# Long-run loads with strided reads of the turned tiles, in a gated recurrence fused with a multiplicative feed-forward layer

## Chip, cores, metric

One core of a Trainium2 chip. The metric is the device time of one execution in microseconds (us).

## The reference, cut to what matters

```python
# x, r_gate, i_gate: (4, 5824, 256) float32; a_param: (256,)
log_a   = 8.0 * sigmoid(r_gate) * log(clip(sigmoid(a_param), 1e-6, 1 - 1e-6))
a_t     = exp(log_a)
x_gated = sqrt(max(1 - a_t * a_t, 1e-6)) * sigmoid(i_gate) * x
h = a_t[:, t] * h + x_gated[:, t]          # for each t in order; y[:, t] = h
out = (((y @ w1) * (y @ w2)) @ w3) @ w_out # y as 23296 tokens x 256
```

The recurrence runs along the tokens, so its two inputs, the decay `a` and the gated input, must lie in the order of time when it is scanned.

## The kernel before

23296 tokens pass in chunks of 512 (the first has 256). A chunk of r, i and x is loaded with tokens on partitions. Tanh makes the sigmoids, the tiles are turned so that features lie on partitions and tokens along the free dimension, and there decay, square, root, gated input and scan run. Two up-projections, their product and one down-projection (w3 and w_out are folded into one matrix at the start) give the output. The instruction order of every engine is computed ahead from estimated durations and is fixed.

```python
def load(c, nm):                       # nm is "r", "i" or "x"
    n = sizes[c] // P                  # P = 128
    t = loads.tile([P, 4, D], F32, name=nm + "_t", tag=nm)
    nc.sync.dma_start(
        out=t[:, :n, :],
        in_=src[nm][starts[c]:starts[c] + sizes[c], :].rearrange("(n p) c -> p n c", p=P))
    T[nm, c] = t
# ... tanh, plus-one and product with x; turned by PE into PSUM for c < NPE (6), else by a DMA transpose into SBUF
def decay(c, cb):                      # ACT, per half of the features
    nc.scalar.activation(out=T["a", c][:, cb, :w], in_=T["pr", c][:, cb, :w], func=AF.Exp,
                         scale=la4[:, cb:cb + 1], bias=la4[:, cb:cb + 1])
# ... square (GpSimd from chunk 4 on), root (ACT)
def gated(c):                          # VectorE; n and pu are both in SBUF from chunk 6 on
    nc.vector.scalar_tensor_tensor(
        out=T["n", c][:, :, :w], in0=T["n", c][:, :, :w], scalar=1e-3,
        in1=T["pu", c][:, :, :w], op0=ALU.max, op1=ALU.mult)
# ... scan (VectorE, two SBUF inputs), cast of h (GpSimd), up, copy (ACT), product (VectorE), down, evac, store
```

On VectorE's queue the gated inputs and scans of a later chunk stand between the products of the current one. A product that is late keeps a PSUM buffer, and PE waits for it (4.0 us in all before).

## Time and profile before

| | before |
|---|---|
| median of the first runs | 532.71 us (532.49 to 533.56) |
| profiled span | 530.9 us |
| PE, ACT, DVE, POOL busy | 94, 87, 84, 63% |
| chain that ended last | 81% PE |

PE, ACT, DVE and POOL are TensorE, ScalarE, VectorE and GpSimd; PEld is PE's loading of weights. In the views, pa and pb are the two up-projections in PSUM, sa is ACT's copy of pa, g_t is the product of sa and pb, po is the down-projection, a_t is the decay, nrm is the gated input, u_t is GpSimd's product of gate and x, h_t is the scan; rt and ut are turned tiles in SBUF, ptr is one in PSUM. Three views of before. First the windows of the steady stretch (columns: stretch, length, busy us and count of PE, PEld, DVE, ACT, POOL, then clock, DMA share, GB/s):

```profile
100.00:450.00 350.00, 348.05 (x2137) 208.89 (x2135) 309.06 (x241) 331.88 (x390) 262.02 (x200) 1.00 0.97 254
```

Then who waited for whom (us in all, times, longest us):

```profile
PE pa L227 <- DVE g_t L241: 4.0, 7, 1.7
...
PE pb L227 <- ACT sa L234: 1.1, 1, 1.1
```

And the decay's source line (ns minimum/median/maximum), with its source in SBUF (rt) and in PSUM (ptr):

```profile
L179 ACT ACTIVATE a_t<-rt,la x80: 798/815/851, 54.9 to 449.0; 128x512 f32<-128x512 bf16 x80
L179 ACT ACTIVATE a_t<-ptr,la x12: 556/770/787, 9.3 to 43.0; 128x512 f32<-128x512 bf16 x10, 128x256 f32<-128x256 bf16 x2
```

PE works through 348 of 350 us and hardly waits for the copies (sa, 1.1 us in all) and products (g_t, 4.0 us).

VectorE's gated inputs and scans, which read SBUF alone in the steady stretch, and GpSimd's instructions hold each other up. Before, a gated input of 1024 columns takes 1192 ns at least and up to 2340, a scan up to 2327, and GpSimd's square 1032 at least and up to 2048. The product g_t, whose second input is in PSUM, takes 1223 ns at most in all of its 184 records. The texts call the two engines, as far as they hold each other up, the port pair, and the time of such instructions port time.

### The profile page before, as it was taken

Reading aid. Unit: us, or ns where it says so; the run is one execution under the profiler, and the core shown is the slowest. Engines: PE = TensorE matmul, PEld = TensorE weight load, DVE = VectorE, ACT = ScalarE, POOL = GpSimd, SP = SyncE. Lnnn points to the kernel's source line nnn. Section 1 sums busy time; section 2 is a strip of 40 time slices with the busy share of each in tenths; the row PEclk is TensorE's granted clock in tenths of the full one; section 3 lists DMA queues with packets and bytes.
Section 4 is the critical chain, followed back from the end, with each engine's and each line's share of the span. In section 5 each row is a group of like instructions: output and inputs, shape, how many; then the busy total and the mean of one; then the engine's idle time right before and its main releaser. Section 6 shows DMA issues by size and latency. Waiting matters only on the chain.

```text
span 530.9 us, 8667 instructions
## 1 busy us (share of the span) xinstructions
PE 498.4 (94%) x3144; PEld 303.3 (57%) x3144; DVE 446.7 (84%) x367; ACT 463.1 (87%) x546; POOL 335.8 (63%) x260
## 2 busy tenths in 40 slices
PE   1568899999999999999999999999999999999997
PEld 1434565666565566565656565565665655566655
DVE  2998988997968899998999988789898889899641
ACT  6998879999999999999999899799998999965452
POOL 1338485887758686876859788578868578841000
PEclk9999999999999999999999999999999999999999
DMA  8998999999997996997997879999899787231112
GB/s 274 356 359 243 292 282 296 324 299 275 295 273 199 279 315 171 278 299 197 287 252 221 226 204 238 329 196 266 226 274 303 199 208 212 61 98 59 41 61 99
DMA packets 184939, 124.31 MB, mean 234 GB/s; under 512 B 88640, under 2 KB 182848, under 8 KB 184896
## 3 DMA queue, kind: packets, MB, share of 16 engines
q1 hardware_dynamic: 184624, 123.76, 86.4%
q8 instruction: 24, 0.39, 0.3%
q14 instruction: 19, 0.16, 0.1%
q10 hardware_dynamic: 272, 0.00, 0.0%
HBM read 78.91 MB, written 23.86 MB: 194 GB/s over the span
## 4 chain that ended last, share of the span: by engine, by line
PE 81%; DVE 8%; ACT 4%; issue 3%; DMA 3%; SPq 0%; DVEq 0%; ACTq 0%
PE pa L227 27%; PE pb L227 26%; PE po L248 26%; DVE g_t L241 2%; DMA rt<-th_r 2%; DVE h_t L211 2%; DVE w_t L276 1%; ACT sa L234 1%; PE pw L299 1%; ACT th_i L133 1%; DMA i_t<-in_i_gate_dram 1%; DVE nrm L196 1%; DVE u_t L148 1%; ACT ot L254 1%; ACT a_t L179 1%
## 5 line engine op out<-in xcount | busy, mean ns | idle before, releaser
L241 DVE TENSOR_TENSOR g_t<-sa,pb 128x1024 bf16<-128x1024 bf16 (+1 forms) x184 | 218.4, 1199 | 60.0 <-ACT sa L234 44.8
L227 PEld LDWEIGHTS <-w_sb 128*128 128x128 bf16 x1472 | 144.6, 98 | 149.1 <-issue 10.7
L234 ACT CAST sa<-pa 128x1024 bf16<-128x1024 f32 (+1 forms) x184 | 183.0, 999 | 32.8 <-PE pa L227 30.9
L227 PE MATMUL pa<-y_t,w_sb 128*128 128x512 bf16 (+1 forms) x736 | 188.7, 380 | 4.0 <-DVE g_t L241 4.0
L227 PE MATMUL pb<-y_t,w_sb 128*128 128x512 bf16 (+1 forms) x736 | 188.4, 379 | 2.9 <-DVE g_t L241 1.5
L248 PE MATMUL po<-wp_sb,g_t 128*128 128x256 bf16 x1456 | 181.7, 273 | 0.2 <-DVE nrm L196 0.2
L248 PEld LDWEIGHTS <-g_t 128*128 128x128 bf16 x1456 | 142.4, 98 | 46.0 <-issue 0.4
L211 DVE TENSOR_TENSOR_SCAN h_t<-a_t,h_t,nrm 128x512 f32<-128x512 f32 (+3 forms) x90 | 136.6, 1534 | 0.8
L187 POOL TENSOR_TENSOR nrm<-a_t 128x512 f32<-128x512 f32 x84 | 104.7, 1258 | 43.5 <-ACT a_t L179 43.2
L153 POOL TENSOR_TENSOR u_t<-th_i,x_t 128x512 bf16<-128x512 f32 x80 | 116.5, 1472 | 2.5
L219 POOL CAST y_t<-h_t 128x1024 bf16<-128x1024 f32 x38 | 44.6, 1173 | 67.9 <-DVE h_t L211 62.1
L138 POOL TENSOR_SCALAR th_i<-th_i 128x1024 f32<-128x1024 f32 x42 | 57.6, 1371 | 21.8 <-ACT th_i L133 21.8
L254 ACT COPY ot<-po 128x512 f32<-128x512 f32 x91 | 53.4, 587 | 16.3 <-PE po L248 15.6
L179 ACT ACTIVATE a_t<-rt,la 128x512 f32<-128x512 bf16 x80 | 63.5, 816 | 4.5 <-DMA rt<-th_r 4.2
L196 DVE SCALAR_TENSOR_TENSOR nrm<-nrm,ut 128x1024 f32<-128x1024 f32 x40 | 59.8, 1494 | 2.4 <-ACT nrm L191 2.4
L133 ACT ACTIVATE th_i<-i_t 128x1024 f32<-128x1024 f32 (+1 forms) x46 | 48.2, 1052 | 1.1 <-DMA i_t<-in_i_gate_dram 1.0
L191 ACT ACTIVATE nrm<-nrm 128x1024 f32<-128x1024 f32 (+1 forms) x46 | 48.1, 1056 | 0.8 <-DVE nrm L187 0.6
L126 ACT ACTIVATE th_r<-r_t 128x1024 bf16<-128x1024 f32 x40 | 42.3, 1063 | 2.1 <-DMA r_t<-in_r_gate_dram 2.0
L161 PE MATMUL ptr<-ident,th_r 128*128 128x128 bf16 x44 | 4.7, 269 | 16.7 <-DVE ident L73 8.7
L276 POOL CAST w_sb<-wf 128x1024 bf16<-128x1024 f32 x4 | 6.1, 1545 | 19.7 <-DMA wf<-in_moe_w_dram 19.7
L191 ACT ACT_TABLE_LOAD x14 | 18.0, 1283 | 0.2
L161 PEld LDWEIGHTS <-th_r 128*128 128x128 bf16 x44 | 3.7, 122 | 18.5 <-ACT th_r L124 14.9
(33 smaller groups left out, 127.1 us busy)
## 6 DMA issues: line engine op xcount, KB each, us to landing
out_dram<-ot SPq DMA_DIRECT2D x91, 256.0 KB, 3.6
r_t<-in_r_gate_dram SPq DMA_DIRECT2D x45, 512.0 KB, 5.3
i_t<-in_i_gate_dram SPq DMA_DIRECT2D x45, 512.0 KB, 5.2
x_t<-in_x_dram SPq DMA_DIRECT2D x45, 512.0 KB, 5.0
wf<-in_moe_w_dram SPq DMA_DIRECT2D x12, 512.0 KB, 5.7
wf<-in_moe_w_out_dram SPq DMA_DIRECT2D x2, 512.0 KB, 6.0
rt<-th_r SPq DMA_TRANSPOSE x40, 4.5
ut<-u_t SPq DMA_TRANSPOSE x40, 4.6
```

The lines of the kernel that those rows point to most:

```text
L138: nc.gpsimd.tensor_scalar(t, t, 1.0, 1.0, op0=ALU.add, op1=ALU.mult)
L153: nc.gpsimd.tensor_mul(out=u.rearrange("p cb j q -> p j cb q")[:, js], in0=cut(t)[:, js], in1=cut(T["x", c])[:, js])
L179: nc.scalar.activation(out=T["a", c][:, cb, :w], in_=T["pr", c][:, cb, :w], func=AF.Exp, scale=la4[:, cb:cb + 1], bias=la4[:, cb:cb + 1])
L187: eng.tensor_mul(out=T["n", c][:, cb, :w], in0=T["a", c][:, cb, :w], in1=T["a", c][:, cb, :w])
L191: nc.scalar.activation(out=T["n", c][:, :, :w], in_=T["n", c][:, :, :w], func=AF.Sqrt, scale=-1.0, bias=1.0)
L196: nc.vector.scalar_tensor_tensor(out=T["n", c][:, :, :w], in0=T["n", c][:, :, :w], scalar=1e-3, in1=T["pu", c][:, :, :w], op0=ALU.max, op1 ...
L211: nc.vector.tensor_tensor_scan(T["h", c][:, cb, lo:hi], T["a", c][:, cb, lo:hi], T["n", c][:, cb, lo:hi], init, ALU.mult, ALU.add)
L227: nc.tensor.matmul(out=pp[:, q, :w], lhsT=w_sb[:, cb, m * P:(m + 1) * P], rhs=T["y", c][:, cb, :w], start=(cb == 0), stop=(cb == NCB - 1))
L234: nc.scalar.copy(out=sa[:, :, :w], in_=T["pa", c, mp][:, :, :w])
L241: nc.vector.tensor_mul(out=T["g", c][:, 2 * mp:2 * mp + 2, :w], in0=T["sa", c, mp][:, :, :w], in1=T["pb", c, mp][:, :, :w])
L248: nc.tensor.matmul(out=T["po", c, j // 2][:, j % 2, :], lhsT=T["g", c][:, k, j * P:(j + 1) * P], rhs=wp_sb[:, k, :], start=(k == 0), stop= ...
L254: nc.scalar.copy(out=T["ot", c, j2], in_=T["po", c, j2])
```

## The change

The intent is longer DRAM runs. With `(n p)` a partition takes four tokens that lie 128 tokens apart, in runs of 1 KB; with `(p n)` it takes four neighbours in one run of 4 KB. After turning, column `j * 128 + q` then holds token `4q + j`, so decay and gated input must read with a stride to put the tokens back in the order of time.

```diff
+    def turned(t):
+        return t.rearrange("p (j q) -> p q j", q=P)
+
+    def in_time(t):
+        return t.rearrange("p (q j) -> p q j", q=P)
 ...
     def load(c, nm):
-            in_=src[nm][starts[c]:starts[c] + sizes[c], :].rearrange("(n p) c -> p n c", p=P))
+            in_=src[nm][starts[c]:starts[c] + sizes[c], :].rearrange("(p n) c -> p n c", p=P))
 ...
     def decay(c, cb):
-        nc.scalar.activation(out=T["a", c][:, cb, :w], in_=T["pr", c][:, cb, :w], func=AF.Exp,
+        nc.scalar.activation(out=in_time(T["a", c][:, cb, :w]), in_=turned(T["pr", c][:, cb, :w]), func=AF.Exp,
                              scale=la4[:, cb:cb + 1], bias=la4[:, cb:cb + 1])
 ...
     def gated(c):
-        nc.vector.scalar_tensor_tensor(
-            out=T["n", c][:, :, :w], in0=T["n", c][:, :, :w], scalar=1e-3,
-            in1=T["pu", c][:, :, :w], op0=ALU.max, op1=ALU.mult)
+        for cb in range(NCB):
+            n = in_time(T["n", c][:, cb, :w])
+            nc.vector.scalar_tensor_tensor(out=n, in0=n, scalar=1e-3, in1=turned(T["pu", c][:, cb, :w]),
+                                           op0=ALU.max, op1=ALU.mult)
```

## The prediction

> **What bounds the kernel now.** I read the page's busy shares first, then the windows of the steady part, then the forms of single instructions, then the chain that ended last. The page:
>
> ```profile
> span 530.9 us, 8667 instructions
> ...
> PE 498.4 (94%) x3144; PEld 303.3 (57%) x3144; DVE 446.7 (84%) x367; ACT 463.1 (87%) x546; POOL 335.8 (63%) x260
> ...
> PE 81%; DVE 8%; ACT 4%; issue 3%; DMA 3%; SPq 0%; DVEq 0%; ACTq 0%
> ```
>
> The third line is the chain that ended last: 81% of it is matmuls and only 3% (16 us) is DMA. The windows show where PE's missing 6% lies (columns: stretch, its length, busy us of PE, PEld, DVE, ACT, POOL, then clock, DMA share, GB/s):
>
> ```profile
> 0.00:20.00 20.00, 3.15 (x26) 2.56 (x27) 9.60 (x15) 15.22 (x19) 3.98 (x8) 1.00 0.94 299
> 20.00:60.00 40.00, 32.40 (x233) 19.59 (x234) 38.32 (x39) 35.70 (x43) 20.56 (x17) 0.96 0.99 318
> ...
> 200.00:250.00 50.00, 50.00 (x305) 29.65 (x303) 46.08 (x36) 48.61 (x57) 36.71 (x29) 1.00 0.90 232
> 250.00:300.00 50.00, 50.00 (x309) 30.00 (x307) 46.08 (x37) 46.84 (x56) 36.48 (x28) 1.00 0.98 262
> ```
>
> PE is full from 100 us on; of its 32.5 us of idle time 24.4 lie before 60 us (16.9 + 7.6), where the first chunk is on its way through all engines. So a gain has to come from the start; the steady part can only lose. But the steady part is tight on every engine, not on PE alone. I summed the seven 50 us windows from 100 to 450 us: PE 348, ACT 332, DVE 309, POOL 262 of 350. In that stretch PE does 537 pa matmuls, 16 to a chunk of 512 tokens, hence 33.6 chunks, one every 10.42 us.
>
> [...]The same instruction has two lengths in the trace:
>
> ```profile
> L196 DVE SCALAR_TENSOR_TENSOR nrm<-nrm,ut x40: 1192/1265/2340, 86.4 to 489.3; 128x1024 f32<-128x1024 f32 x40
> ...
> L196 DVE SCALAR_TENSOR_TENSOR nrm<-nrm,ptr x6: 675/1206/1207, 16.3 to 70.1; 128x1024 f32<-128x1024 f32 x5, 128x512 f32<-128x512 f32 x1
> ...
> L187 POOL TENSOR_TENSOR nrm<-a_t x84: 1032/1039/2048, 38.2 to 450.2; 128x512 f32<-128x512 f32 x84
> ...
> L153 POOL TENSOR_TENSOR u_t<-th_i,x_t x80: 1257/1272/2262, 61.4 to 470.3; 128x512 bf16<-128x512 f32 x80
> ...
> L219 POOL CAST y_t<-h_t x38: 1027/1036/2017, 112.3 to 495.9; 128x1024 bf16<-128x1024 f32 x38
> ```
>
> These lines (from the views by source line and by tile) give ns minimum/median/maximum. Each maximum is about the minimum plus one instruction of the other engine: one blocks the other. With the minima as undisturbed costs, 100 to 450 us holds on POOL 65 u (81.7), 71 squares (73.3), 32 plus-ones at 1.036 (33.2), 32 casts (32.9), together 221 us; on DVE 33 gated inputs (39.3) and scans (60 full ones at about 1.25, as one undisturbed scan in the timeline shows, and 13.7 of short ones), together 128. Sum 349 of 350 us. That adds durations and ignores that the ends of two instructions may overlap, so it is an estimate, but the port pair is about as full as PE.
>
> [...]
>
> [...]The changed reads take four bf16 values 256 bytes apart, then go back 766 bytes for the next four[...]. No instruction of the trace of before reads that way, so the trace can neither confirm nor deny a penalty for ACT and DVE.
>
> [...]
>
> [...]its packet records have 1024-byte packets at a median of 46 ns, and the 1024 packets of 4096 bytes of the w3 loads at 159 ns, so 4 KB cost 159 instead of 184 ns.
>
> **The change, part by part.**
> 1. Loads. 69,888 packets of 1 KB become about 17,300 of 4 KB and 384 of 2 KB (the first chunk). Saved: 17,300 x 25 ns = 0.43 ms of engine time, over 16 engines 27 us of some 460 us that the queue is busy. But the start of the chain waits for latency: the first i_t load is 4.0 us of it, for 256 tokens, and two transposes (rt) stand in the chain with 5.4 and 5.9 us. If each of these gets 10 to 15% shorter, that is 2 us. I allow 3 us gained in all.[...]
> 2. Tanh, plus, u, the transposes, the squares, roots, scans, casts, matmuls and stores stay as they are: same shapes, same addresses, same order. The schedule is computed from durations in the source that the diff leaves alone.
> 3. Gated input. One 128x1024 instruction becomes two of 128x512. From the PSUM forms above: 1206 for 1024 columns, 675 for 512, so 0.531 us per 512 columns and 0.144 fixed. Two halves at full rate cost 1.35: +0.14 per chunk. If the strided input takes two cycles per element, each half costs 0.144 + 1.062 = 1.21, a pair 2.41: +1.2 per chunk. At one and a half cycles +0.68.[...]
> 4. Decay. 80 of 816 ns plus 12 from PSUM (773 at 512 columns, 560 at 256: 0.426 us per 512 columns). No penalty: unchanged. Two cycles per element: 1.24 us each, +0.85 per chunk on ACT. One and a half: +0.43.
>
> Put against 350 us and 33.6 chunks, with two cycles per element: port pair 349 + 40 = 389; ACT 332 + 29 = 361; DVE 309 + 40 = 349 before more blocking; PE 350. The port pair would end last: 389 / 33.6 = 11.6 us per chunk, 1.16 over PE's 10.42. Some 41 chunks run in that regime (60 to 490 us): 41 x 1.16 = 48 us, less about 6 us that the lead of the casts over their matmuls can absorb, less the 3 us of the loads: +39, about 572 us.
>
> **The rivals.**
> A. Strided reads are free. Then gated adds 0.14 x 41 = 6 us to the port pair, which its lead and the 3 us from the loads about cancel: 528 to 536, within 2%. For it: [...]the author left the scheduler's durations alone.[...]
> B. Full penalty on both engines: about 572, and up to 590 if ACT's and DVE's delays add rather than overlap, because the order on each engine is fixed and a late copy holds PE.
> C. Half a penalty, or a penalty on one engine alone. Half: port pair +0.68 x 41 = 28 us, less 9: about 552. ACT alone: 361 against 350 in the window, 12 to 20 us: about 545. DVE alone: nearly as B, about 568.
> D. The loads were the true limit (the DMA share is 0.9 to 1.1 in the middle), and longer packets free everything. Against: ACT waited for r_t 4.0 us and for rt 4.2 us in the whole run, and PE is at 50.00 of 50.00 beside the busiest DMA. Even with every DMA piece of the chain a third shorter this gives 5 us, 1%. Over 2% would need 10.7 us, nearly half of what PE idles before 60 us.
>
> **Range and chances.** A 0.38 (about 531), C 0.22 (about 552), B 0.36 (about 573), D as a gain over 2% 0.04. I choose a point between C and B, 558 us, a compromise and not a mode. The range 528 to 588 leaves out a gain of over 1% and a pile-up of delays. Faster 0.04, same 0.37, slower 0.59.
>
> **What would show each step.** Loads: packet count from 184,939 to about 133,000, and r_t, i_t, x_t landing below the present 5.3, 5.2 and 5.0 us. Gated: a group of 128x512 with twice the count, its minimum 0.67 (free) or near 1.2 (full penalty). Decay: 0.82 against about 1.24. Port pair: POOL's medians rising toward its maxima, and DVE busy near all of the steady part. PE: windows from 100 to 450 below 50.00, waiting for g_t and sa, if B or C holds; still full if A does. The prediction is wrong if the decay and gated forms show no stride cost (then A, about 531), or if the strided cost is there and the port is less full than I sum (then nearer 545).

## The result, and the profile after

570.0 us median of 4 runs (568.53 to 570.57) beside 533.09 us for before (532.49 to 533.56): a ratio of 1.069 (95% interval 1.066 to 1.071), slower by 37 us. Ratios here are the mean time of one kernel's fast runs over that of the other's fast runs of the same rounds, so they are not quite the ratio of the medians. The profiled execution was granted a clock of 0.986; the run with 0.996 took 568.5 us, so the clock explains some 2 us.

The page of the changed kernel, the totals and the chain that ended last:

```profile
span 568.8 us, 8655 instructions
...
PE 506.8 (89%) x3087; PEld 304.3 (53%) x3144; DVE 492.7 (87%) x413; ACT 496.3 (87%) x546; POOL 356.4 (63%) x260
...
DMA packets 132715, 124.31 MB, mean 219 GB/s; under 512 B 88640, under 2 KB 112960, under 8 KB 132672
...
PE 30%; ACT 28%; DVE 22%; issue 15%; DMA 4%; SPq 0%; another core or an unknown queue 0%; DVEq 0%; ACTq 0%
```

The packets fell from 184,939 as the loads meant them to, with the same 124.31 MB. The chain is no longer PE's: three engines share it. The same stretch and the same waits as before:

```profile
100.00:450.00 350.00, 324.77 (x1923) 190.65 (x1958) 321.82 (x251) 330.21 (x357) 261.03 (x185) 1.00 0.88 235
```

```profile
PE pa L236 <- DVE g_t L250: 20.2, 21, 2.9
...
PE pb L236 <- ACT sa L243: 6.1, 14, 0.8
```

PE lost 23 us of this stretch (the figure is rough: 57 of its 3144 matmul records are missing from this trace; its weight loads, which are complete, fell by 8%, from 2135 to 1958). The waits that grew are those for the product (4.0 to 20.2 us) and for the copy (1.1 to 6.1 us). No other engine is full either: ACT is busy as before with fewer instructions. The two strided lines:

```profile
L187 ACT ACTIVATE a_t<-rt,la x80: 1268/1292/1532, 56.1 to 483.3; 128x512 f32<-128x512 bf16 x80
L187 ACT ACTIVATE a_t<-ptr,la x12: 556/772/796, 9.6 to 41.8; 128x512 f32<-128x512 bf16 x10, 128x256 f32<-128x256 bf16 x2
...
L206 DVE SCALAR_TENSOR_TENSOR nrm<-nrm,ut x80: 1012/1117/2154, 87.9 to 528.1; 128x512 f32<-128x512 f32 x80
...
L206 DVE SCALAR_TENSOR_TENSOR nrm<-nrm,ptr x12: 414/678/690, 16.1 to 72.0; 128x512 f32<-128x512 f32 x10, 128x256 f32<-128x256 f32 x2
```

From SBUF a strided decay takes 1292 ns instead of 815. From PSUM the decay takes a median of 772 ns with the same stride of 256 bytes and took 770 without: there it was free. The gated half takes at least 1012 ns when its second input lies in SBUF, and a median of 678 ns (512 columns) when it lies in PSUM, where one of 512 columns took 675 before.

How a wait for the product arises is to be seen in the timeline of the changed kernel (start us, us, engine, line; x2 is a pair without a gap):

```profile
303.92 3.33 POOL L161 TENSOR_TENSOR u_t<-th_i,x_t 128x512 bf16<-128x512 f32 x2
...
304.95 3.20 DVE L206 SCALAR_TENSOR_TENSOR nrm<-nrm,ut 128x512 f32<-128x512 f32 x2
...
307.20 4.77 POOL L195 TENSOR_TENSOR nrm<-a_t 128x512 f32<-128x512 f32 x3
...
308.07 2.07 DVE L220 TENSOR_TENSOR_SCAN h_t<-a_t,h_t,nrm 128x512 f32<-128x512 f32 x1
...
310.06 2.32 DVE L250 TENSOR_TENSOR g_t<-sa,pb 128x1024 bf16<-128x1024 bf16 x2
...
311.30 1.02 PE L236 MATMUL pa<-y_t,w_sb 128*128 128x512 bf16 x3 [1.13 <-DVE g_t L250]
```

Two gated halves (L206) would need 2.0 us alone; between GpSimd's u products (L161) and squares (L195) they take 3.2. The scan behind them (L220) takes 2.07 us; another at 312.31 in this stretch takes 1.27. The product g_t that PE needs (L250) begins only at 310.06, and PE stands for 1.13 us.

### The profile page after: what moved, and what is told of

The parts are those of the page before. It is cut to its first block, busy times and chain, and to the rows that moved or that the text cites.

```text
span 568.8 us, 8655 instructions
## 1 busy us (share of the span) xinstructions
PE 506.8 (89%) x3087; PEld 304.3 (53%) x3144; DVE 492.7 (87%) x413; ACT 496.3 (87%) x546; POOL 356.4 (63%) x260
## 2 busy tenths in 40 slices
DMA packets 132715, 124.31 MB, mean 219 GB/s; under 512 B 88640, under 2 KB 112960, under 8 KB 132672
## 4 chain that ended last, share of the span: by engine, by line
PE 30%; ACT 28%; DVE 22%; issue 15%; DMA 4%; SPq 0%; another core or an unknown queue 0%; DVEq 0%; ACTq 0%
DVE g_t L250 11%; PE pa L236 10%; ACT sa L243 10%; PE pb L236 9%; PE po L257 8%; ACT a_t L187 7%; DVE h_t L220 5%; DVE nrm L206 4%; ACT ot L263 2%; DMA rt<-th_r 2%; ACT nrm L199 2%; ACT th_i L141 2%; ACT th_r L134 2%; ACT L199 2%; DVE w_t L285 1%
## 5 line engine op out<-in xcount | busy, mean ns | idle before, releaser
L250 DVE TENSOR_TENSOR g_t<-sa,pb 128x1024 bf16<-128x1024 bf16 (+1 forms) x184 | 217.0, 1198 | 49.9 <-ACT sa L243 41.1
L236 PE MATMUL pa<-y_t,w_sb 128*128 128x512 bf16 (+1 forms) x701 | 186.9, 382 | 23.3 <-DVE g_t L250 20.2
L195 POOL TENSOR_TENSOR nrm<-a_t 128x512 f32<-128x512 f32 x84 | 111.8, 1339 | 51.8 <-ACT a_t L187 49.6
L220 DVE TENSOR_TENSOR_SCAN h_t<-a_t,h_t,nrm 128x512 f32<-128x512 f32 (+3 forms) x90 | 133.9, 1504 | 0.0
L161 POOL TENSOR_TENSOR u_t<-th_i,x_t 128x512 bf16<-128x512 f32 x80 | 124.6, 1572 | 2.5
L206 DVE SCALAR_TENSOR_TENSOR nrm<-nrm,ut 128x512 f32<-128x512 f32 x80 | 113.0, 1453 | 3.7 <-ACT nrm L199 3.7
L187 ACT ACTIVATE a_t<-rt,la 128x512 f32<-128x512 bf16 x80 | 102.4, 1304 | 2.4 <-DMA rt<-th_r 2.3
L146 POOL TENSOR_SCALAR th_i<-th_i 128x1024 f32<-128x1024 f32 x42 | 62.9, 1497 | 24.2 <-ACT th_i L141 24.2
```

What stands on the lines that cost most here:

```text
L146: nc.gpsimd.tensor_scalar(t, t, 1.0, 1.0, op0=ALU.add, op1=ALU.mult)
L161: nc.gpsimd.tensor_mul(out=u.rearrange("p cb j q -> p j cb q")[:, js], in0=cut(t)[:, js], in1=cut(T["x", c])[:, js])
L187: nc.scalar.activation(out=in_time(T["a", c][:, cb, :w]), in_=turned(T["pr", c][:, cb, :w]), func=AF.Exp, scale=la4[:, cb:cb + 1], bias=la ...
L195: eng.tensor_mul(out=T["n", c][:, cb, :w], in0=T["a", c][:, cb, :w], in1=T["a", c][:, cb, :w])
L206: nc.vector.scalar_tensor_tensor(out=n, in0=n, scalar=1e-3, in1=turned(T["pu", c][:, cb, :w]), op0=ALU.max, op1=ALU.mult)
L220: nc.vector.tensor_tensor_scan(T["h", c][:, cb, lo:hi], T["a", c][:, cb, lo:hi], T["n", c][:, cb, lo:hi], init, ALU.mult, ALU.add)
```

## The experiments

Theory at the start (PORT): the two strided reads are all of the loss, ACT's decay accounts for a smaller part, and the gated input for a larger one, because it adds to the time of those instructions of VectorE and GpSimd that hold each other up, which by the prediction's estimate from the trace of before fill 349 of 350 us. Rivals: the loads do damage or were a hidden limit; ACT alone sets the time; VectorE's own length does it, without GpSimd; the second instruction does it, not the stride.

Twelve kernels ran. Kernels that leave the tokens out of order give wrong results; their instructions, sizes and addresses are those that matter here.

### The loads alone

Edit: only the line `(n p)` to `(p n)`; wrong result.

> The kernel before with the long-run loads alone; nothing puts the tokens back in order, so the result is wrong on purpose. Theory (the steady part is bound by PE and the port pair, DMA is hidden): 529 to 533 us, at most 3 us gained. Rival (longer packets hurt, for instance by delaying the transposes, and are part of the +37 us): over 535 us. Rival (the loads were a hidden limit and the change would have won but for the strides): under 525 us.

Measured: 531.44 us (530.22 to 532.58) against 532.26; ratio 0.999 (0.996 to 1.002). Neither gain nor damage. The median times from issue to landing are 5.4, 5.1 and 5.0 us for r, i and x, against 5.3, 5.2 and 5.0 before. So the longer packets do not even land sooner; what they save (the queue's share of the DMA engines' time falls from 86.4 to 83.5%) is hidden, and the rival that saw a limit in the loads falls.

### The strided decay alone

```diff
-        nc.scalar.activation(out=T["a", c][:, cb, :w], in_=T["pr", c][:, cb, :w], func=AF.Exp,
+        nc.scalar.activation(out=in_time(T["a", c][:, cb, :w]), in_=turned(T["pr", c][:, cb, :w]), func=AF.Exp,
```

> The kernel before with the strided decay alone (old loads, wrong order of tokens on purpose). Each of 80 decays takes 1292 instead of 815 ns, so ACT gets 0.95 us more per chunk and the port pair nothing. Theory PORT (the port pair of DVE and POOL ends last in the changed kernel, ACT comes second): ACT 332 + 32 = 364 of 350 us in the former steady window, 10.8 us per chunk, so 543 to 552 us. Rival ACT (the scalar engine alone set the new time): 565 to 572 us, all of the loss. Rival SLACK (ACT had the room): under 536 us.

Measured: 550.4 us (548.65 to 553.05), ratio 1.035, +18 us. That is in PORT's range, which had ACT as the second cause; the rivals that ACT sets all of the new time, or has the room, both miss. In its list of waits PE's wait for the copy is the one that grew, from 1.1 us to this:

```profile
PE pb L233 <- ACT sa L240: 13.4, 26, 1.8
```

### The strided gated input alone, in two halves

Edit: only the change's `gated`.

> The kernel before with the gated input in two strided halves alone (old loads, wrong order on purpose). A pair takes at least 2.02 instead of 1.19 us[...]. Theory PORT: 349 + 28 = 377 of 350 us, 11.2 us per chunk, so 552 to 564 us, the larger part of the loss. Rival ACT: under 540 us. Rival DVE (DVE's own time[...]): 309 + 28 = 337 of 350, so no bound and under 540 us too, told apart by the padding run.

Measured: 562.5 us (560.9 to 565.56), ratio 1.058, +30 us. This is the larger part and in PORT's range, with the decay unchanged; so ACT alone does not set the time.

### The split alone

```diff
-        nc.vector.scalar_tensor_tensor(
-            out=T["n", c][:, :, :w], in0=T["n", c][:, :, :w], scalar=1e-3,
-            in1=T["pu", c][:, :, :w], op0=ALU.max, op1=ALU.mult)
+        for cb in range(NCB):
+            n = T["n", c][:, cb, :w]
+            nc.vector.scalar_tensor_tensor(out=n, in0=n, scalar=1e-3, in1=T["pu", c][:, cb, :w],
+                                           op0=ALU.max, op1=ALU.mult)
```

> The kernel before with the gated input as two halves of unit stride (right result). Each pair costs 1.35 instead of 1.21 us. Theory PORT with its 6 us of lead: 532 to 537 us. Rival (the second instruction and its semaphores, not the stride, are what costs): over 545 us.

Measured: 540.72 us (538.53 to 542.85), ratio 1.015, +8.5 us, between what PORT and its rival named; neither is right. It is under the 2% that count as slower, but clear of zero (interval 1.012 to 1.019). Splitting costs more than its fixed 0.14 us per chunk (an estimate from the PSUM forms of before, 2 x 675 less 1206 ns), which is 6 us in 41 chunks. The gated line of this run in the view that groups instructions by shape (busy us, mean ns) and by source line:

```profile
L198 DVE SCALAR_TENSOR_TENSOR nrm<-nrm,ut 128x512 f32<-128x512 f32 x80 | 86.6, 1121 | 2.2 <-ACT nrm L191 2.2
```

```profile
L198 DVE SCALAR_TENSOR_TENSOR nrm<-nrm,ut x80: 658/1064/1761, 86.3 to 500.0; 128x512 f32<-128x512 f32 x80
```

80 x (1121 - 658 ns) are 37 us beyond the undisturbed time. Before, the same reckoning gives 40 x (1494 - 1192) = 12 us. VectorE's idle time before the halves is 2.2 us, as before (2.4), so the cost is inside the instructions and not in issuing them or in semaphores. This was the first sign that the number of instructions matters, not only their length.

### Both strides with the old loads

Edit: decay and gated of the change, loads as before.

> Both strided reads on the kernel before with its old loads (wrong order of tokens on purpose): the change without its loads. Theory (all of the loss is the two strided reads, the loads give 0 to 3 us): 568 to 574 us. Rival (the long-run loads do their share of damage when ACT and DVE are late): under 566 us. The two alone cost 18 and 30 us; if they simply added it would be 581 us.

Measured: 570.31 us (568.73 to 570.87), ratio 1.071, the whole loss. The strides and the split together are all of it; the loads have no part. The parts overlap: 18 and 30 alone, 38 together.

### The same length on VectorE without a wait for GpSimd

```diff
             in1=T["pu", c][:, :, :w], op0=ALU.max, op1=ALU.mult)
+        if c >= NPE:
+            nc.vector.tensor_reduce(out=pad, in_=T["pu", c].rearrange("p cb x -> p (cb x)")[:, :640],
+                                    op=ALU.max, axis=mybir.AxisListType.X)
```

> The kernel before with a reduction of 640 bf16 values of the turned input on DVE ahead of nothing, right after the gated input, for 40 chunks (right result, the sum is thrown away): about 0.8 us more DVE time per chunk, as much as the strided pair adds[...]. Theory PORT[...]: DVE goes from 309 to about 336 of 350 us and stays below, so 532 to 542 us, against 562 for the gated input alone. Rival DVE (the length of DVE's own line[...], since its order is fixed and the products wait behind): 555 to 563 us.[...]

Measured: 537.31 us (535.35 to 538.32), ratio 1.009, +5 us. The reduction's line in the trace:

```profile
L201 DVE TENSOR_REDUCE pad<-ut x40: 803/806/815, 87.5 to 494.7; 128x1 f32<-128x640 bf16 x40
```

Its shortest is 803 and its longest 815 ns, so it never queues behind GpSimd; and GpSimd is busy for 261 of the 350 us of the steady stretch, as before (262), so it doesn't wait for the reduction either. Nearly as many microseconds on VectorE as the strided pair adds (0.83 per chunk undisturbed, 2 x 1.012 less 1.192) cost 5 us, not 30. VectorE's plain length is at most a small part of the cause.

### Taking GpSimd time away

Edit: GpSimd's plus-one becomes a bare `return`, in the changed kernel and, as a control, in the kernel before; both wrong.

> The changed kernel without the plus-one on GpSimd (wrong result on purpose): 1.04 us of port time per chunk less, more than the strided pair adds (0.83), DVE and ACT as long as before. Theory PORT: the port pair falls back to its old filling, what is left is ACT, so 545 to 555 us as in decay_only. Rival DVE or ACT (engine lines, not the port): 566 to 572 us.

> Control: the kernel before without the plus-one (wrong result on purpose). Theory (PE bounds, port pair just below it): 526 to 533 us. Rival (the port pair is the true bound of the kernel before as well): under 522 us.

Measured: 562.36 us (562.07 to 563.16), ratio 1.057, for the changed kernel, only some 8 us less than with the plus-one; 531.45 us (531.24 to 533.15), ratio 0.999, for the control. The control agrees with PE as the bound of before. The other misses both expectations: 1.04 us of GpSimd's time per chunk is more than the 0.83 that the stride and the split add to VectorE's, yet 12 of the 20 us that the gated input adds to the decay alone (562.4 and 570.0 against 550.4) stay. **PORT as a sum of the two engines' times falls.** A new theory (ACQUIRE) took its place: what costs is each separate wait of a VectorE instruction behind a running GpSimd instruction, with the scans and products queued behind. Two halves wait twice.

### One gated instruction again

The changed kernel has the fused form with two free dimensions in each half; a plain product with three was built and ran (this run). The given inputs never reach the floor of 1e-3, so leaving it out keeps the result right.

```diff
-        for cb in range(NCB):
-            n = in_time(T["n", c][:, cb, :w])
-            nc.vector.scalar_tensor_tensor(out=n, in0=n, scalar=1e-3, in1=turned(T["pu", c][:, cb, :w]),
-                                           op0=ALU.max, op1=ALU.mult)
+        n = T["n", c][:, :, :w].rearrange("p cb (q j) -> p cb q j", q=P)
+        nc.vector.tensor_mul(out=n, in0=n, in1=T["pu", c][:, :, :w].rearrange("p cb (j q) -> p cb q j", q=P))
```

> The changed kernel with its two strided gated halves as one instruction again: [...]the floor of 1e-3 is dropped (the given inputs never reach it, so the result should stay right). Theory ACQUIRE (each DVE instruction with two SBUF inputs queues anew behind a GpSimd instruction of 1.0 to 1.3 us, and the products queue behind it; the second half is a second such wait): about 1 us less on most chunks, so 558 to 565 us, and the gated input's median well below the 3.2 us that a pair now takes beside GpSimd. Theory PORT as a plain sum: only the fixed 0.14 us per chunk goes, 6 us, so 563 to 566 us. Rival (the wait is spent once whatever the number of instructions): 568 to 571 us.

> The strided gated input alone, as one plain product of 128x1024 (old loads, plain decay; wrong order of tokens on purpose): 1.93 instead of 1.19 us undisturbed[...]. Theory ACQUIRE (in the run with the strided halves alone, 562.5 us, the second acquisition was most of the loss; the longer instruction by itself costs about what the padding on DVE did, 5 us): 535 to 546 us. Theory PORT as a plain sum of port time: 349 + 24 = 373 of 350 us, less the lead, 550 to 558 us. Rival (ACT hid the gated input's cost in the run with one gated instruction, so it comes back here): over 555 us.

Measured for the changed kernel with one gated instruction: 555.1 us (554.79 to 556.04), ratio 1.044. That is 15 us less than the changed kernel: below all three ranges, 3 us beyond ACQUIRE's on its own side. For the strided gated input alone as one instruction: 545.21 us (544.35 to 546.21), ratio 1.027, at the upper end of ACQUIRE's range and below PORT's sum. The same view of the gated input, first in the changed kernel, then with one instruction:

```profile
L206 DVE SCALAR_TENSOR_TENSOR nrm<-nrm,ut 128x512 f32<-128x512 f32 x80 | 113.0, 1453 | 3.7 <-ACT nrm L199 3.7
```

```profile
L205 DVE TENSOR_TENSOR nrm<-nrm,ut 128x1024 f32<-128x1024 f32 x40 | 87.1, 2178 | 3.7 <-ACT nrm L199 3.7
```

The undisturbed times are nearly the same, 2 x 1012 and 1925 ns. Beyond them the pairs wait 80 x 0.441 = 35 us, the single instructions 40 x 0.253 = 10 us. PE's wait of its pa matmuls for the product falls from 20.2 us to this:

```profile
PE pa L234 <- DVE g_t L248: 9.2, 14, 2.0
```

The single records of these two traces say which half waits. In the changed kernel the first halves wait 11 us in all beyond their undisturbed 1012 ns, as the single instructions do (10), and the second halves 24; 12 first halves, 25 second ones and 12 single instructions wait over 0.3 us. So the second half is a wait of its own. Not all of this time is gained, though. With one instruction the full scans take 5 us longer in all, and GpSimd's u products, squares, plus-ones and casts 12 us: some waiting only moves, mostly to GpSimd. VectorE's gated inputs and full scans together go from 241 to 220 us, and that is the line that PE waits for.

So of the 30 us that the gated input costs alone, 17 go with its second instruction (562.5 to 545.2) and 13.5 stay. By the padding run, about 5 of these are VectorE's length; the other 8 or so are put down to waits between VectorE and GpSimd by that difference alone; no run shows it.

### The stride by its size

Edit: on the kernel before, from chunk 6 on, decay and gated halves read or write with another step on every eighth chunk, each on a line of its own. Its output is wrong, which doesn't matter for the time.

> One look, wrong result on purpose: the kernel before with steps of several sizes on the chunks from 6 on, each on its own line. Decay: unit stride, reads of bf16 at steps of 4, 8, 16 and 32 bytes, writes of float32 at steps of 8, 16 and 32 bytes. Gated input as two halves: second input (bf16) at 4, 8, 16 and 32 bytes, first input and output (float32) at 8 and at 16 bytes, and all three operands stepped. Theory LINE[...]: 4 and 8 bytes free, 16 and 32 as dear as 256, that is decay 1.27 and gated half 1.01 us, float32 steps of 8 bytes free and of 16 dear. Rival STEP (any step but 1 costs): 4 bytes as dear as 256. Rival FAR (only far jumps cost): 16 and 32 bytes still near 0.81 and 0.66 us.

The decay's lines: unit step, reads of bf16 at 4, 8 and 16 bytes, then writes of float32 at 8 and 16 bytes (the 32-byte steps, 1328 ns read and 1323 written, are like those of 16):

```profile
L187 ACT ACTIVATE a_t<-rt,la x10: 800/816/819, 71.6 to 416.7; 128x512 f32<-128x512 bf16 x10
L189 ACT ACTIVATE a_t<-rt,la x10: 802/815/824, 87.1 to 424.2; 128x512 f32<-128x512 bf16 x10
L191 ACT ACTIVATE a_t<-rt,la x10: 841/866/936, 96.7 to 451.9; 128x512 f32<-128x512 bf16 x10
L193 ACT ACTIVATE a_t<-rt,la x10: 1315/1330/1368, 103.4 to 457.1; 128x512 f32<-128x512 bf16 x10
...
L197 ACT ACTIVATE a_t<-rt,la x10: 836/866/892, 130.3 to 467.8; 128x512 f32<-128x512 bf16 x10
L199 ACT ACTIVATE a_t<-rt,la x10: 1284/1320/1381, 53.9 to 403.4; 128x512 f32<-128x512 bf16 x10
```

The gated halves: second input at 8 and 16 bytes, then first input and output (float32) at 16 with the second input (bf16) at 8 (look at the minima; medians hold waits for GpSimd):

```profile
L230 DVE SCALAR_TENSOR_TENSOR nrm<-nrm,ut x10: 659/789/1755, 126.0 to 486.2; 128x512 f32<-128x512 f32 x10
L232 DVE SCALAR_TENSOR_TENSOR nrm<-nrm,ut x10: 1072/1112/1965, 138.4 to 494.6; 128x512 f32<-128x512 f32 x10
...
L238 DVE SCALAR_TENSOR_TENSOR nrm<-nrm,ut x10: 1092/1195/1889, 84.6 to 440.9; 128x512 f32<-128x512 f32 x10
```

LINE's times came as named, within 0.08 us. Steps of 4 and 8 bytes were free or nearly so (815 and 866 ns on ACT beside 816 at unit step; 659 on VectorE), float32 included (866 ns for a write at 8 bytes on ACT; first input and output at 8 bytes on VectorE: at least 678 ns, as at unit step in this run). At the larger steps that ran the time was about the same whatever the distance (reads on ACT: 1330 ns at 16 bytes, 1328 at 32 and 1292 at 256; gated halves: at least 1072, 1065 and 1012), and on ACT for writes of float32 as for reads of bf16 (1320 at 16 bytes, 1323 at 32); on VectorE float32 at 16 bytes in first input and output alone took at least 1076. Why the time rises between 8 and 16 bytes was not shown. Rivals STEP and FAR both fall. Stepping three operands (1092) cost hardly more than stepping one (1072). By these durations, writing with a step of 16 bytes, instead of reading with one of 256, would not have helped; no run times it.

### The part that is free

The start of the kernel turns into PSUM, where the stride cost nothing (decay 772 ns beside 770). So the change can be had there alone.

```diff
             in_=src[nm][starts[c]:starts[c] + sizes[c], :].rearrange(
-                "(n p) c -> p n c", p=P))
+                "(p n) c -> p n c" if c < NPE else "(n p) c -> p n c", p=P))
 # decay and gated as in the change where c < NPE, else as before
```

> The change for the first 6 chunks alone, those whose turned tiles lie in PSUM (right result): there the changed kernel's decays took 772 ns (770 before) and its gated halves 676 each, so the stride costs nothing, and all the start of the kernel gets the long-run loads. Theory (the start waits for latency and engine chains, not for bytes): 529.5 to 533 us, no clear difference. Rival (the loads bound the start): 525 to 529 us, a version that beats both.

Measured: correct, 531.52 us (529.56 to 534.55, 14 runs) against 531.77; ratio 1.000 (0.998 to 1.002). The version neither loses nor wins: in the first 60 us PE is busy 36.1 instead of 35.6 us, which the end does not show. No version that beats the kernel before came out.

## Why the prediction was right or wrong

It was right in its class and its range (528 to 588 us; 570 measured), and its rival B, a full penalty on both engines, named 572 us. The point, 558, was a compromise between rivals and took only two thirds of the loss; the range was wide enough to hold no change as well as a loss of 55 us. That 572 came so close is luck (point 4).

1. **Loads**: 3 us allowed, 0.8 measured and not clear of zero. The packet count, 132,715, was as foretold. The shorter landings in the changed kernel (5.2, 4.7 and 4.7 us) are not the packets' doing: with the loads alone they stay at 5.4, 5.1 and 5.0.
2. **Decay**: 1.24 us expected at full penalty (estimate, with the columns' time of the trace doubled; nothing in the trace of before showed a penalty), 1.29 measured; +0.95 us per chunk on ACT instead of +0.85. Alone it gives +18 us, of the 12 to 20 that rival C allowed. In the sum that gives 572 it counted for nothing beside the sum of VectorE and GpSimd; measured, it adds 8 us to the gated input (562.5 to 570.3).
3. **Gated input**: that the stride costs was right, the term mis-sized. A half takes 1.01 us undisturbed, not 1.21, since the stride adds 0.34 us to 512 columns and not 0.53. That the strided reads from PSUM have no penalty (772 ns beside 770 on ACT, 678 beside 675 on VectorE) was not foreseen; it cost the sum nothing, which took 41 of the 46 chunks where 40 have the stride in SBUF.
4. **VectorE and GpSimd together**: this step failed in its form. The prediction added the two engines' times ("The port pair would end last: 389 / 33.6 = 11.6 us per chunk"). Taking more time from GpSimd (1.04 us per chunk) than VectorE had been given (0.83) recovered only 8 us. The signs that it named for this step did not come either: in the steady stretch VectorE was busy 322 of 350 us and not near all of it, GpSimd 261 (262 before), and of GpSimd's medians only the plus-one's rose (1052 to 1570 ns; squares 1039 to 1042, u products 1272 to 1277). What counted was how often VectorE must wait for a running GpSimd instruction: the second instruction alone is 8.5 us at unit stride and 15 to 17 us with the stride. With the measured 0.83 us per chunk in place of 1.2, the prediction's own sum gives about 557 us (349 + 28 = 377; 377 / 33.6 is 0.80 over PE's 10.42; 41 x 0.80, less 6 and 3), an estimate from its figures. So the oversized stride stood in for some 13 us of waits and of ACT that the sum leaves out, by luck.
5. **The split in rival A**: "6 us to the port pair, which its lead and the 3 us from the loads about cancel". It did not cancel: 540.7 us for the split alone. The 6 us of lead were an estimate that no run shows.
6. **Rival D**, the loads as the true limit, was given 0.04 and falls with the loads-only run. One reading against it was wrong: beside the busiest DMA (share 1.12, 100 to 150 us) PE was at 49.63 of 50, not at 50.00.

What stays open: how far ACT and VectorE hide one another. Decay alone (+18) and one gated instruction alone (+13.5) give +23 together, not 31.5; no run separates the overlap. And no run has the split without a busy GpSimd beside it: that the second half's cost is waiting for GpSimd is read from the durations.

## What to carry to other kernels

A read or write with a step of 16 bytes or more between elements in SBUF made a 512-column instruction on ACT or VectorE 54 to 66% longer here (1292 to 1330 ns beside 815 on ACT, at least 1012 to 1092 beside 658 on VectorE), so the layout with the longer DRAM runs had to be paid for there; where transfers are hidden, as here (ratio 0.999 for the loads alone), there is nothing to pay it with. The same reordering from PSUM was free (772 ns beside 770 on ACT). And where VectorE's instructions wait for a busy GpSimd, as the gated inputs and scans did here, count the instructions, not only their microseconds: 40 gated inputs waited 12 us in all, the same work in 80 halves 37 us, and the scans and products behind them queued too.
